# First batch's q loaded as rows of 34 tokens, and x put back in order on its way out of PSUM

## The chip, the cores and the metric

The kernel runs on one core of a Trainium2 chip. A core has TensorE (PE in the profile, with its weight loads shown as PEld), VectorE (DVE), ScalarE (ACT), GpSimd (POOL) and the queues that issue DMA transfers, here those of SyncE (SPq) and ScalarE (ACTq). The metric is the device time of one execution in microseconds; lower is better.

## The reference

Two blocks follow each other, for 4 batches of 1088 tokens. The first is a sketched linear attention with 4 heads of 32 columns:

```python
def phi(x):                       # S1, S2: 8 x 32, float64 in the inputs
    a = einsum('rd,bhsd->bhsr', S1, x)
    b = einsum('rd,bhsd->bhsr', S2, x)
    return einsum('bhsi,bhsj->bhsij', a, b)      # 64 features per token and head
q_p, k_p = phi(q), phi(k)
kv  = einsum('bhsf,bhsd->bhfd', k_p, v)
z   = sum(k_p, axis=2)
x   = einsum('bhsf,bhfd->bhsd', q_p, kv) / (einsum('bhsf,bhf->bhs', q_p, z) + 1e-6)
```

The four heads are laid side by side, so x is 1088 x 128 per batch. The second block is a mixture of 4 attention experts:

```python
logits = x @ w_gate                              # the two largest of 4 are chosen
w = softmax over the two chosen logits
for e in range(4):
    a = causal_softmax((x @ wq[e]) @ (x @ wk[e]).T / 8)
    out += (w of e, 0 where e is not chosen) * (a @ (x @ wv[e]) @ wo[e])
```

## The kernel before, in words

Every piece of work is a *job*: a function that issues a few instructions on one engine, with what it reads, what it makes and which buffers it holds. `ORDER` (line 22 on) is a list of job numbers written out by hand; `Plan.run` goes through it and issues the jobs in that order, so each engine's instruction stream, and each DMA queue's, is the list cut down to that engine. A letter behind a number picks one of two engines; a dummy matmul with a "b" is left out. Buffers of a pool are handed out in order of the list: there are four PSUM pairs (two banks each), three buffers for loaded and turned q and k, three for features, six general ones.

For each batch the work goes:

1. *Load* k, q, v. For batch 0 k comes as rows of 34 tokens: partition 32h + t holds tokens 34t to 34t + 33 of head h, each 32 columns, in two transfers of 2,048 and 2,304 bytes a partition (L424). q comes by head, in four transfers on two queues: partition t of a head holds tokens t, 32 + t, 64 + t and so on, in 34 runs of 128 bytes (`by_head`, L429). v of batch 0 comes as rows of 34 tokens too (L436, L440).
2. *Turn* (DVE): 32 x 32 blocks are transposed, so that the columns of a head stand on partitions. k's turn for batch 0 also puts the tokens in another order, with strided reads and writes of 256 columns (L489); q's goes straight (L495).
3. *Sketch* (PE, L519): 32 matmuls with 32 x 32 weights and 288 columns, for S1 and S2, four heads and four groups. Then DVE brings the result *back* (L523).
4. *Features* (DVE and POOL, L528): the 64 products, four jobs for q and four for k.
5. *Sums* over the tokens for k (PE, L559), kept by ACT or DVE.
6. For batch 0 (`attend_rows`): q's features are turned by PE in five pieces (L593) and copied out (L192), *numer* multiplies them with the sums (L616), *divide* divides on DVE (L623 to L625), *turn x* transposes x in three pieces (L631) and *keep x* copies each out of PSUM (L192). *Store x* writes each piece to DRAM (L644, L647) and *fetch x* reads it back in rows of 32 partitions for the values (L651).
7. *Choose experts*: logits by thirds (L808), turned back (L812), comparisons, choices (L833 to L849) and shares.
8. *Queries* (L961, base copies and predicated picks L974), *scores* (L999), exp (L1027), weights (POOL, L1042), turn (L1047), *values* (L1075), *outputs* (L1196).

The sketch matrices come as float64 and are decoded by integer operations on DVE (L303 to L318); PE meanwhile runs dummy matmuls on a zeroed tile (L248). Batch 1's preparation is interleaved with batch 0's choices and scores, and so on. Line 192 is the copy helper of all engines.

Of the kernel before, what the change touches and what calls it, by code (L numbers as in the profile page):

```python
# [10 lines left out]
F32 = mybir.dt.float32  # L11
# [10 lines left out]
1 16a 60 9a 13a 22a 24a 27a 77 5b 46 31a 12a 0 3 2 45 48 79 76 78 90 4 49 75 81 83 74 89 52 51 88 80 87 8a 50 98 99 47  # L22
64 54 100 91 102a 104a 84 101a 92 93 82 53 391 96a 103b 66 97a 19b 95a 85b 113 114a 94b 109 110a 393 59 117 118a 56
111 394 65 392 402 44a 55 115 86a 106 57 112b 63 105 67a 401 405 116b 395 58 108b 406 407 411a 397 399 107a 119 398
404 120 124 125 129 126 127a 130 400 121 61 7b 408a 122a 396 68 131 62a 146 132a 409a 412 147 70 410a 413 414a 69 150
148 403 71 152 153 151 154 149 169 415 128 167 416 420a 123 687 168 170 417 418a 155 17b 179 686 685 684 694 133 73 72
419a 162 163 180 184b 421 174 175 183a 164 422 424 423 430 425 426 139 156 157a 185 158 159a 182 181 246 245 186 187
194 431 137 171 172 249a 188 189 695 208 209 210 195 428a 427a 432 434a 433a 196 250a 222 223 688 160 161a 26b 25b 38b
201 165 429 202 224 203 319 215 197a 190b 251 198 216 225a 226 435 166a 199 200 247 227 248 698 252 228 268 204b 191
192 205 206 217 218a 219 176 220 135 173 700 699 267 269 270 318 323a 193 322a 436 438a 207 141 703a 271b 704b 437b  # L30
324 221 211a 212 260 261 262 263a 213 275 321 276 277 278 279b 177 178b 214 253 254 456 458 272 457 273 14b 142 693
320 325 255 292 291 293 274 701a 42b 264 691 280 702a 134 136 229 230 231 459 460 692 256b 234a 284 294 283 233a 462
281 257 232a 258 265 690 689 706 705 285 286 235b 342 707a 708 237 236 239 709 710 696 713a 238 711a 712a 259 282 697
461 266 295a 296 343 326 344 297 287a 327 328 288 289 298 714 715 717 463 350 290 329 330b 716 723 724 725 345 346a
10b 143 21b 472 138 331 473 477b 718 347 351 352 35b 353 354a 144 727a 332 348 719 140 29b 439 476b 464 299 300 301
302 303 304 308a 441 306a 307a 726a 333 349 467 478 335 310 474 440 334 305b 309 475 336 479 359 337 338a 358 360 339
361 362 355 468 508 509 442 720a 984 311 312 540 721a 363 340 501 364a 443 502 480 979 341 481 482 541 314 465 487 365
488 356 357 483a 315 313 366 367 538 494 977 978 495 980 316a 981 728 539 542a 368 369 370 987 496 503 504a 145 371
372 373 374 317 469 375 470 543a 544 545 471a 505 506 985 988 484 485 486 497b 444 498 722 499 510 511b 489 490a 491
512 513 376 379b 447 500 380a 515 383 516 553 377a 381 445 554 492 493 378a 382 448 584 585 586 517 518a 729 555 449  # L40
446 453 982 983 730a 514 519 731b 451 991 520 521 993 749 556b 992 994b 587 588a 569 546 996b 750 384 385 997a 507 557
558 547 751 548 386 568 989 522 589 523 524 549a 550 551 559 570 571 526a 752 753 590 242 591 525a 754 611 529 995a
530 241 528b 527a 531 612 616a 561 760 732 452 387 615a 755 455 466 733 572a 756 560 573 574 389 614 562 563 986 613
240 576 577 617 618 620 575 43b 552 532 644 619 578 28b 18b 579 621 243a 580b 581 643 765 652 564a 565 766 769a 582
651 768 757 645 583 636 566 567 390 653 770a 771 635 654 655 627 622 244 623a 761 762 628 637 656 657b 629 630 638 767
772 624 658 659 646 625 592 660 639a 640 631b 641 593 594 450 595 596 597 794 598a 999 647a 632 642 601b 602 648 600a
599a 795 633 634 649 998 736 1000a 603 605 535 626 454 773 774 787 650 534 763 788 533 780 781 808 809 810 811a 764a
536b 812 661 662 789 775 663 813 796 797b 798 790b 604 782 664 665 666 667 1002 814 668 669 990 1005a 734 776b 777
672a 671a 778 1006b 670b 1001 735 739 1003 832 1004a 791 388 799 783b 800 673a 674 675 831 835a 801 784 1007 802 803
1008 792 676 1009 793 836a 834 677 1010 1016 833 904 738 678 742 758 804b 1011 837 30b 1017 785 805 806 759 1012 1018  # L50
838 1013a 905 908a 862 1014a 1020a 909a 807 679 910 878 786 779 737 537 877 879 747 839 840 841 907 906 880 911 861
863 1019a 1021 881b 842a 846 847 682 740 815 816 817 746 864 865a 820a 853 866 867 821a 824 854 1015 868 882 936 819a
823 855 39b 34b 40b 41b 848 849b 937 818a 850 851 856 822 938 1022 1024b 869 1023b 607 843 883 884 939 870 748 871 872
# [62 lines left out]
def kernel(  # L116
# [177 lines left out]
    def decode():  # L294
# [8 lines left out]
        ve.tensor_scalar(out=ex, in0=hi, scalar1=20, scalar2=0x7FF, op0=SHR, op1=AND)  # L303
# [3 lines left out]
        ve.tensor_single_scalar(lw, lo, 29, op=SHR)  # L307
        ve.tensor_single_scalar(ex, ex, 255, op=ALU.min)
        ve.tensor_tensor(out=ma, in0=ma, in1=lw, op=OR)
        ve.tensor_single_scalar(S_hi, ex, 0, op=ALU.is_gt)  # L310
        ve.tensor_single_scalar(lw, lo, 0x1FFFFFFF, op=AND)
        ve.tensor_single_scalar(ex, ex, 23, op=SHL)
        ve.tensor_copy(last, lw)
        ve.tensor_tensor(out=sg, in0=sg, in1=ex, op=OR)
        ve.tensor_tensor(out=ma, in0=ma, in1=sg, op=OR)
        ve.scalar_tensor_tensor(out=S_lo, in0=last, scalar=2.0**-52, in1=sg.bitcast(F32), op0=ALU.mult, op1=ALU.mult)
        ve.tensor_tensor(out=S_hi, in0=ma.bitcast(F32), in1=S_hi, op=ALU.mult)
# [8 lines left out]
    job("decode", "DVE", 2.3, lambda e: decode(), ["raw"], "ST", [sroom], rank=-190)  # L326
# [89 lines left out]
    def prepare(b, rank):  # L416
# [3 lines left out]

        def load_k(eng, x):
            if early:
                c0, c1 = (0, 512, S)[x : x + 2]
                eng.dma_start(out=plan[kin][:, c0:c1], in_=k[b].rearrange("h (t c) d -> (h t) (c d)", c=C)[:, c0:c1])  # L424
            else:
                by_head(eng, plan[kin], k, x)
# [31 lines left out]
        for x in range(2 if early else 4):  # L458
            job(f"load k{b}.{x}", "SP", 0.45 if early else 0.7, lambda e, x=x: load_k(nc.sync, x), lead,
                ("kin", b, x if early else 0), [kin], landing=0.8 if early else 0.95, rank=rank(-0.1))  # L460
        def load_rows():

            nc.sync.dma_start(out=plan[qin][:, 0:S], in_=q[b].rearrange("h (t c) d -> (h t) (c d)", c=C))

        if early:
            for x in range(4):
                job(f"load q{b}.{x}", "ACT" if x % 2 else "SP", 0.42, lambda e, x=x: by_head(nc.scalar if e == "ACT" else nc.sync, plan[qin], q, x),
                    lead, ("qin", b), [qin], landing=0.85, rank=rank(-0.09))
# [10 lines left out]
        def turn_k(x):  # L479
# [8 lines left out]
            for g in range(2):  # L488
                nc.vector.transpose(d[:, :, 2 * x + g], s[:, :, 2 * x + g])  # L489
# [796 lines left out]
```

## Time and profile before

| | |
|---|---|
| median of 3 runs | 277.88 us (277.2 to 278.68) |
| profiled execution | 277.85 us, span 276.1 us |
| PE busy | 261.8 us (95%) |
| DVE busy | 217.5 us (79%) |
| POOL busy | 153.8 us (56%) |
| ACT busy | 99.4 us (36%) |
| DMA | 85,579 packets, 27.36 MB, 54,112 packets under 512 bytes |

Engine rows give the time in which an engine had an instruction in flight; waiting for something else is idle time, shown in brackets behind a row with what ended it. Matmul records come in pairs for each float32 matmul. SPq and ACTq rows are the issue of a transfer; the time to landing is given in the DMA rows. The chain of waits follows the work that ended last back to the start.

### The profile page before, as it was taken

Reading aid. Unit: us, or ns where it says so; the run is one execution under the profiler, and the core shown is the slowest. Engines: PE = TensorE matmul, PEld = TensorE weight load, DVE = VectorE, ACT = ScalarE, POOL = GpSimd, SP = SyncE. Lnnn points to the kernel's source line nnn. Section 1 sums busy time; section 2 is a strip of 40 time slices with the busy share of each in tenths; the row PEclk is TensorE's granted clock in tenths of the full one; section 3 lists DMA queues with packets and bytes.
Section 4 is the critical chain, followed back from the end, with each engine's and each line's share of the span. In section 5 each row is a group of like instructions: output and inputs, shape, how many; then the busy total and the mean of one; then the engine's idle time right before and its main releaser. Section 6 shows DMA issues by size and latency. Waiting matters only on the chain.

```text
span 276.1 us, 9491 instructions
## 1 busy us (share of the span) xinstructions
PE 261.8 (95%) x3961; PEld 193.7 (70%) x3961; DVE 217.5 (79%) x543; ACT 99.4 (36%) x271; POOL 153.8 (56%) x247
## 2 busy tenths in 40 slices
PE   7679998899999999989999999999999999999994
PEld 2367854457585796676589986665597975789994
DVE  3998689989989987998969437989899358995344
ACT  2030356344423444333462332462532425434110
POOL 5386358656789834546565448666348242652730
PEclk9999999999999999999999999999999999999999
DMA  7965739952607979143900165700412854940012
GB/s 158 183 144 82 156 91 205 165 72 60 125 20 116 193 193 170 37 103 68 198 6 4 30 151 130 176 2 2 101 47 51 154 121 104 171 81 2 5 32 52
DMA packets 85579, 27.36 MB, mean 99 GB/s; under 512 B 54112, under 2 KB 84896, under 8 KB 85536
## 3 DMA queue, kind: packets, MB, share of 16 engines
q1 hardware_dynamic: 83168, 26.41, 48.0%
q8 instruction: 31, 0.51, 0.8%
q10 hardware_dynamic: 2368, 0.35, 0.7%
q14 instruction: 12, 0.10, 0.1%
HBM read 22.22 MB, written 4.52 MB: 97 GB/s over the span
## 4 chain that ended last, share of the span: by engine, by line
PE 63%; DVE 22%; DMA 4%; issue 4%; ACT 3%; POOL 2%; SPq 1%; DVEq 0%; ACTq 0%; POOLq 0%
PE pair L1075 24%; PE pair L999 18%; PE pair L961 6%; PE pair L1196 6%; DVE AT L1047 3%; DVE w L1011 2%; DVE w L523 2%; DVE fp L528 2%; DVE qs L974 2%; DMA in<-in_k_dram 2%; DMA xra<-xd 2%; PE pair L1146 2%; PE pair L559 2%; PE pair L519 1%; PE pair L1172 1%
## 5 line engine op out<-in xcount | busy, mean ns | idle before, releaser
L1042 POOL TENSOR_SCALAR w<-w,rs,sh 128x896 f32<-128x896 f32 (+15 forms) x68 | 55.9, 829 | 55.0 <-DVE rs L1038 53.0
L999 PE MATMUL pair<-xT,qs 128*128 128x384 f32 (+11 forms) x216 | 76.4, 481 | 3.4 <-DVE agg L192 1.3
L1027 ACT ACTIVATE w<-w,mx 128x640 f32<-128x640 f32 (+15 forms) x68 | 52.4, 771 | 69.2 <-DVE mx L1011 54.1
L999 PEld LDWEIGHTS pair<-xT,qs 128*128 128x128 f32 x216 | 37.4, 190 | 28.7 <-issue 9.7
L1047 DVE STREAM_TRANSPOSE AT<-w 128x576 f32<-128x576 f32 (+14 forms) x68 | 50.7, 758 | 5.9 <-POOL w L1042 5.5
L1011 DVE CUSTOM_DVE_ANT_0 w<-pair,mask 128x768 f32<-128x768 f32 (+13 forms) x68 | 48.1, 719 | 6.5 <-PE pair L999 6.1
L1075 PEld LDWEIGHTS pair<-AT,xra 32*128 32x128 f32 x1136 | 41.6, 185 | 6.4 <-DVE mx L1011 2.6
L1075 PE MATMUL pair<-AT,xra 32*128 32x192 f32 (+5 forms) x1136 | 44.7, 303 | 0.2 <-DMA xra<-xd 0.2
L1102 POOL TENSOR_TENSOR agg<-agg,mb 128x768 f32<-128x768 f32 (+1 forms) x22 | 34.1, 1561 | 11.7 <-ACT agg L192 6.6
L961 PE MATMUL pair<-xT,Mq 128*128 128x384 f32 (+1 forms) x96 | 34.8, 476 | 0.3 <-DVE w L523 0.2
L528 POOL TENSOR_TENSOR fp<-w 128x576 f32<-128x576 f32 x23 | 27.1, 1194 | 8.2 <-DVE w L523 8.0
L192 ACT COPY agg<-pair 128x384 f32<-128x384 f32 (+1 forms) x34 | 14.5, 462 | 44.3 <-PE pair L1075 36.7
L1075 PE MATMUL pair<-AT,xrb 32*128 32x160 f32 (+5 forms) x752 | 26.9, 287 | 0.0
L1075 PEld LDWEIGHTS pair<-AT,xrb 32*128 32x128 f32 x752 | 26.4, 185 | 0.5 <-issue 0.4
L961 PEld LDWEIGHTS pair<-xT,Mq 128*128 128x128 f32 x96 | 17.3, 190 | 11.2 <-issue 3.1
L974 DVE COPY_PREDICATED qs<-mb,pair 128x768 f32<-128x768 uint16 (+1 forms) x24 | 23.0, 959 | 2.2 <-DMA mb<-md 1.4
L1196 PEld LDWEIGHTS pair<-Mo,agg 128*128 128x128 f32 x168 | 20.6, 192 | 2.4 <-issue 1.3
L1196 PE MATMUL pair<-Mo,agg 128*128 128x128 f32 x168 | 21.6, 278 | 0.0
L192 DVE COPY agg<-pair 128x384 f32<-128x384 f32 (+1 forms) x12 | 6.4, 533 | 12.7 <-PE pair L1075 7.6
L1035 POOL TENSOR_SCALAR rs<-zs 128x1 f32<-128x1 f32 x31 | 6.6, 213 | 17.0 <-ACT w L1027 13.9
L1098 DVE COPY_PREDICATED agg<-mb,pair 128x384 f32<-128x384 uint16 (+1 forms) x24 | 12.6, 547 | 4.0 <-ACT agg L192 3.9
L1038 DVE RECIPROCAL rs<-rs 128x1 f32<-128x1 f32 x68 | 8.8, 143 | 7.8 <-POOL rs L1035 5.9
(165 smaller groups left out, 308.5 us busy)
## 6 DMA issues: line engine op xcount, KB each, us to landing
mb<-md SPq DMA_DIRECT2D x7, 576.0 KB, 5.4
xrb<-xd SPq DMA_DIRECT2D x16, 192.0 KB, 3.9
xra<-xd SPq DMA_DIRECT2D x16, 192.0 KB, 4.7
xrc<-xd SPq DMA_DIRECT2D x16, 160.0 KB, 4.3
mb<-md SPq DMA_DIRECT2D x4, 480.0 KB, 4.9
in<-in_k_dram SPq DMA_DIRECT2D x12, 136.0 KB, 4.2
in<-in_q_dram SPq DMA_DIRECT2D x3, 544.0 KB, 6.0
xd<-w SPq DMA_DIRECT2D x12, 136.0 KB, 3.6
```

The source lines that it names most:

```text
L192: (nc.scalar.copy if eng == "ACT" else VEC[eng].tensor_copy)(o, i)
L528: VEC[e].tensor_tensor(out=f, in0=a[:, :, None, R : 2 * R].to_broadcast([128, NJ, R, R]), in1=a[:, :, 0:R, None].to_broadcast([128, NJ, R, ...
L961: nc.tensor.matmul(plan[ps[x]][:, y, 0:w], Mq[:, ((1, 2), (0, 3))[x][y]], plan[xT][:, 64 * t0 : 64 * t1], start=True, stop=True)
L974: nc.vector.copy_predicated(chosen(), rows(c), rows(plan[ps[x]]))
L999: nc.tensor.matmul(plan[p][:, y, 0 : c1 - c0], plan[qs][:, 128 * t : 128 * t + 128], plan[xT][:, c0:c1], start=True, stop=True)
L1011: nc.vector.tensor_tensor_reduce(out=o, in0=src, in1=msk, scale=-1.0, scalar=mx[:, b, i, x - 1 : x] if x else 3e38, op0=ALU.add, op1=ALU.m ...
L1027: nc.scalar.activation(out=a, in_=a, func=ACTF.Exp, bias=mx[:, b, i, last : last + 1], scale=-1.0, accum_out=zs[:, b, i : i + 1])
L1042: nc.gpsimd.tensor_scalar(out=a, in0=a, scalar1=rs[:, b, i : i + 1], scalar2=plan[("sh", b)][:, i : i + 1], op0=ALU.mult, op1=ALU.mult)
L1047: nc.vector.transpose(dst[:, 0 : keys // 32, t], plan[A][:, 0:keys].rearrange("p (j s) -> p j s", s=32))
L1075: nc.tensor.matmul(plan[Vk[g // 2]][:, g % 2, lo : 32 * nt], plan[(f"xr{j // 12}", b)][rows, j % 12], a[rows, j, lo:], start=(j == 0), sto ...
L1102: nc.gpsimd.tensor_tensor(out=a, in0=a, in1=plan[mb][:, 2 * x : 2 * x + 2, 0:w], op=ALU.mult)
L1196: nc.tensor.matmul(plan[p][0:m, 0, 128 * x : 128 * x + 128], plan[agg][:, e, 128 * x : 128 * x + m], Mo[:, e], start=(e == 0), stop=(e == ...
```

## The change

- q of batch 0 is loaded like k, as rows of 34 tokens, in two transfers, one on SP's queue and one on ACT's; k's second half moves to ACT's queue.
- The turns of k and q are both plain 512 and 576 column transposes in the order in which the data comes. The tokens of a group then stand in another order, and the sketch of batch 0 is issued in two cuts, one of 32 columns and one of 256, for k and for q.
- x therefore comes out with partition 32g + t, tile j holding token 34t + 8g + j. `keep x` writes it in token order with strided writes (one copy for the first two pieces, two for the last), and all logits wait for all three pieces.
- `store x` is four transfers by group (runs of 4 KB) and one job with two transfers for the last two tokens of each 34, all behind all three divides; each fetch of x waits for all stores.
- The decode of the sketch matrices has 13 instructions in place of 16.
- The first part of `ORDER` is new; from about job 420 of 1275 in the list it is the same. Six dummies are issued in place of ten. The mask is made later on POOL, all five copies of q's turned features are on ACT, the first memsets on DVE change places.

```diff
+        ve.tensor_scalar(out=ma, in0=hi, scalar1=0xFFFFF, scalar2=3, op0=AND, op1=SHL)
         ve.tensor_scalar(out=sg, in0=hi, scalar1=31, scalar2=31, op0=SHR, op1=SHL)
-        ve.tensor_scalar(out=ma, in0=hi, scalar1=0xFFFFF, scalar2=3, op0=AND, op1=SHL)
...
+        ve.scalar_tensor_tensor(out=sg, in0=ex, scalar=23, in1=sg, op0=SHL, op1=OR)
...
+        def by_rows(eng, dst, src, x):
+            c0, c1 = (0, 512, S)[x : x + 2]
+            eng.dma_start(out=dst[:, c0:c1], in_=src[b].rearrange("h (t c) d -> (h t) (c d)", c=C)[:, c0:c1])
...
-            job(f"load k{b}.{x}", "SP", 0.45 if early else 0.7, lambda e, x=x: load_k(nc.sync, x), lead,
+            job(f"load k{b}.{x}", ("SP", "ACT")[x] if early else "SP", 0.45 if early else 0.7,
+                lambda e, x=x: load_k(nc.scalar if e == "ACT" else nc.sync, x), lead,
...
-            for x in range(4):
-                job(f"load q{b}.{x}", "ACT" if x % 2 else "SP", 0.42, lambda e, x=x: by_head(...
+            for x in range(2):
+                job(f"load q{b}.{x}", ("SP", "ACT")[x], 0.42, lambda e, x=x: by_rows(...
...
-            s = src[:, 0 : 128 * N8].rearrange("p (g j d) -> p j g d", g=4, j=N8)
-            d = dst[:, 0 : 128 * N8].rearrange("p (j g t) -> p j g t", j=N8, g=4)
-            for g in range(2):
-                nc.vector.transpose(d[:, :, 2 * x + g], s[:, :, 2 * x + g])
+            cols = slice(512 * x, S if x else 512)
+            nc.vector.transpose(dst[:, cols], src[:, cols])
...
+            if early:
+                cuts = [(32 * N8, 32, lambda a, g: a[:, 128 * N8 + 32 * g : 128 * N8 + 32 * g + 32]),
+                        (0, 32 * N8, lambda a, g: a[:, 32 * N8 * g : 32 * N8 * g + 32 * N8])]
+            for o, w, part in cuts:
+                for s in range(2):
+                    for h in range(H):
...
         def keep_x(e, x0, x1, t):
+            o = plan[xT].rearrange("p (t c) -> p c t", c=C)
+            src = plan[t][:, 0, 0:384].rearrange("p (j g t) -> p j g t", g=4, t=32)
+            n = min(x1, N8) - x0
+            copy(e, o[:, 0 : 4 * N8].rearrange("p (g j) t -> p j g t", g=4)[:, x0 : x0 + n], src[:, 0:n])
+            if x1 > N8:
+                copy(e, o[:, 4 * N8 :], src[:, n, 0 : C - 4 * N8])
+
+        def store_x(g):
+            dst, x = xd[b].rearrange("(t c) d -> t c d", c=C), plan[xs].rearrange("p (j d) -> p j d", d=128)
+            nc.sync.dma_start(out=dst[:, N8 * g : N8 * g + N8], in_=x[32 * g : 32 * g + 32, 0:N8])
+
+        def store_last():
+            dst, x = xd[b].rearrange("(t c) d -> t c d", c=C), plan[xs].rearrange("p (j d) -> p j d", d=128)
+            for g in range(C - 4 * N8):
+                nc.sync.dma_start(out=dst[:, 4 * N8 + g], in_=x[32 * g : 32 * g + 32, N8])
...
-                    [("xd", b, piece[n])], ("xr", b, n), [(f"xr{n}", b)], landing=1.1, rank=at + 0.3)
-        pieces_of[b] = piece
+                    [("xd", b)], ("xr", b, n), [(f"xr{n}", b)], landing=1.1, rank=rank(0.9 + 0.1 * n))
+        pieces_of[b] = {n: 0 for n in range(3)}
```

More of the change, by code (lines that the diff above doesn't have):

```diff
@@ L27 @@
[L27 to L31, printed above, removed]
@@ L325 @@
     job("mask", "POOL", 1.2, lambda e: make_mask(), (), "mask", rank=-60)
-    job("decode", "DVE", 2.3, lambda e: decode(), ["raw"], "ST", [sroom], rank=-190)
+    job("decode", "DVE", 2.0, lambda e: decode(), ["raw"], "ST", [sroom], rank=-190)
     for h in range(1, 4):
@@ L465, in prepare @@
         if early:
[L466 to L468 removed]
+            for x in range(2):
+                job(f"load q{b}.{x}", ("SP", "ACT")[x], 0.42, lambda e, x=x: by_rows(nc.scalar if e == "ACT" else nc.sync, plan[qin], q, x),
+                    lead, ("qin", b, x), [qin], landing=0.8, rank=-198.5)
         else:
[L470 removed]
+            job(f"load q{b}", "SP", 0.45, lambda e: load_rows(), lead, ("qin", b, 0), [qin], landing=3.2, rank=rank(-0.09))
         for x in range(5):
```

139 lines of the change are left out of this document (58 added, 81 removed).

## The prediction

> **What bounds the kernel now.** I read first the stages (busy time of each engine per stretch), because a change to the first batch can only pay where TensorE (PE) has room.
>
> ```profile
> 0.00:6.60 6.60, 5.35 (x18) 2.02 (x18) 2.39 (x20) 1.73 (x3) 3.58 (x22) 1.00 0.79 157
> 6.60:33.40 26.80, 21.48 (x443) 16.58 (x443) 22.13 (x49) 5.12 (x14) 14.60 (x20) 1.00 0.73 137
> 33.40:61.40 28.00, 25.41 (x304) 13.93 (x300) 25.80 (x77) 13.76 (x41) 18.11 (x42) 1.00 0.83 141
> 61.40:276.10 214.70, 209.55 (x3205) 161.12 (x3204) 167.14 (x399) 78.82 (x213) 117.51 (x165) 1.00 0.41 87
> ```
>
> Columns: stretch, length, busy PE, its weight loads, DVE, ACT, POOL, granted clock, DMA share, GB/s. Up to 6.6 us PE runs only dummy matmuls. From 6.6 to 33.4 it idles 26.80 - 21.48 = 5.3 us, from 33.4 to 61.4 another 2.6 us, and then it is 97.6% busy to the end. From the queries of batch 1 on (about 76 us) every engine's order is unchanged. So what counts is how much earlier PE has finished the same work at that point; the rest slides along.
>
> The second view is the chain that ended last, over the start.
>
> ```profile
> 4.60 4.98 DMA in<-in_k_dram
> ...
> 11.70 3.82 DVE fp L528 x3
> ...
> 15.57 0.66 PE pair L593 x4
> ...
> 16.26 0.66 PE pair L593 x4
> ...
> 19.55 0.77 DVE in L483
> ...
> 21.56 1.48 PE pair L519 x55
> ```
>
> The start hangs on k's second transfer (issued 4.60, landed 9.60), since DVE turns k before it takes q's sketch back, and then on DVE's features and copies. The third is the timeline of the start and the steps after it.
>
> ```profile
> 0.91 0.27 DVE L241 MEMSET idle<- 128x256 uint32 x1 [0.91 <-PEq L1270]
> 1.24 5.35 PE L248 MATMUL pair<-idle 128*128 128x512 bf16 x18 [1.24 <-DVE warm L238]
> 1.27 0.41 SPq L234 DMA_DIRECT2D w<-in_S_dram  x1
> 3.42 0.29 DVE L303 TENSOR_SCALAR w<-w 32x32 int32<-32x32 int32 x1 [2.17 <-DMA w<-in_S_dram]
> 5.25 0.23 DVE L318 STREAM_TRANSPOSE SK<-w 32x64 f32<-32x64 f32 x1
> 6.54 1.37 DVE L495 STREAM_TRANSPOSE in<-in 128x576 f32<-128x576 f32 x2 [1.06 <-DMA in<-in_q_dram]
> 7.96 1.62 PE L519 MATMUL pair<-in,SK 32*32 32x288 f32 x64 [1.37 <-DVE in L495]
> 11.85 1.53 POOL L528 TENSOR_TENSOR fp<-w 128x576 f32<-128x576 f32 x1 [4.39 <-DVE w L523]
> 15.57 2.23 PE L593 MATMUL pair<-ident,fp 128*128 128x128 f32 x14 [2.64 <-DVE fp L528]
> 16.90 2.72 DVE L528 TENSOR_TENSOR fp<-w 128x576 f32<-128x576 f32 x3
> 18.82 2.47 PE L559 MATMUL pair<-vp,fp 128*64 128x33 f32 x72
> 23.09 4.23 PE L616 MATMUL pair<-kvz,fp 128*128 128x66 f32 x36
> 24.66 4.58 POOL L528 TENSOR_TENSOR fp<-w 128x576 f32<-128x576 f32 x4 [2.24 <-DVE w L523]
> 33.41 0.71 PE L394 MATMUL pair<-AT 64*128 64x128 f32 x8
> ```
>
> **The change part by part.** q's 4352 runs of 128 B become 256 runs of 2 KB and more. The DMA rows that price them:
>
> ```profile
> in<-in_k_dram SPq DMA_DIRECT2D x1, 288.0 KB, 4.9
> in<-in_q_dram SPq DMA_DIRECT2D x2, 136.0 KB, 3.6
> ```
>
> *Sketch matrices.* The big memset of the dummies' operand moves behind the small one the S loads wait for: issue at 1.27 - 0.27 = 1.0, arrival 3.42 - 0.27 = 3.15. The decode loses 3 of 16 instructions; 3.42 to 5.48 was 2.06 us, so 1.67 now: done at 4.8 instead of 5.5.
>
> *q and k.* q's halves are issued behind S on two queues at about 1.45 and 1.75. Bounds for a row transfer: the 3.6 us of the old q pieces and the 4.9 us of k's 288 KB half, which ran behind other traffic. With little ahead of it I take 3.6: q is in at 5.1 (6.7 at worst). The two turns (1.37) with the small copy end at 6.6, against 7.9. k's first half is issued fourth on SP, at about 2.35, and with 4.9 us is in at 7.25; its turns become contiguous (0.35 us less of DVE). They end at 8.65, under q's sketch.
>
> *The sketches of q and k.* Each is now cut in two: 64 records of 256 columns and 64 more of 32. The present 64 took 1.62 us; less the last one's 0.40 that is 19.2 ns a record.
>
> ```profile
> L519 PE MATMUL pair<-in,SK x224: 401/401/426, 8.0 to 37.5; 32*32 32x288 f32 x112
> ```
>
> If the records are paced by issue, the added 64 cost 64 x 19.2 = 1.23 us; if by columns, nothing (64 x (256 + 32) is the old sum). Nearer is the issue price, since the weight loads double too: q's sketch runs 6.65 to 9.5. The sketch of q is on the path; k's mostly waits for DVE anyhow. For the same step the Trainium skill ("TensorE: Matmul & The Clock Gate", section "Wait — 56ns, not 53.3ns?") says that start-to-start never drops below about 25 ns however few the columns. The 19.2 ns above are already below that, so row and page differ; by the page the 128 records would take 3.2 us and the gain below would shrink by some 0.7 us.
>
> *Features.* DVE takes q's second half back at 9.5 to 10.2 and then runs 2 features instead of 3 before k's turn, POOL two. With POOL busy beside it a DVE feature takes 3.82 / 3 = 1.3 us, and POOL's takes 1.53. DVE: 10.2, feature to 11.5, back to 12.2, feature to 13.5; POOL ends at 13.7. q's features are complete at 13.7, against 15.5. k: backs to 14.9, two features at 1.1 (between 0.91 = 2.72 / 3 and 1.3) to 17.1; POOL's two end at 16.6. Against 16.90 + 2.72 = 19.6 that is 2.5 us earlier.
>
> *Turns, sums, numerators.* The five turns of q's features need PSUM pairs that k's backs free (14.2, 14.9), so they run 13.9 to 16.7; all five copies go to ACT, idle then, which takes two copies off DVE. The sums follow, the last half from 17.1 on, to 19.1 (before 21.3). Batch 1's k turns (0.77 us the one in the chain) no longer stand between copies, so its sketch runs at once, 19.1 to 20.7, and the numerators 20.7 to 24.95 (before 27.3). The last divide ends 1 us behind them, at 25.95.
>
> *x out of PSUM in order.* The copies now write with a stride of 34 words, as batch 1's already do:
>
> ```profile
> L192 ACT COPY xT<-pair 128x512 f32<-128x512 f32 x1 | 1.1, 1130 | 0.0
> L192 ACT COPY fp<-pair 128x512 f32<-128x512 f32 x2 | 1.2, 586 | 10.6 <-PE pair L593 10.5
> L192 DVE COPY xT<-pair 128x64 f32<-128x64 f32 x1 | 0.3, 293 | 0.0
> ```
>
> 1130 against 586 ns for 512 columns: about 1.06 ns more a column. The last piece (256 + 64 columns) takes 0.38 (half of 586, with the fixed part) + 256 x 1.06 ns + 0.29 = 0.94 us on ACT. All logits now wait for all three pieces: turn 0.55, copy 0.94, ready at 27.5. The three logits take 1.4 us to 28.9, and batch 1's sums (2.3) end at 31.2; they need POOL's four features of k1 (4.58 us), which start when k1's first half is back (21.4, behind its sketch) and have two constant jobs of some 2.5 us among them: 28.5, just in time. Before, PE had done this very set when it began L394 at 33.41. So PE is **2.2 us ahead** here. Storing x also becomes all or nothing (six transfers, 4 KB runs), but from 26 us; the fetches serve the values' sums only at 61 us.
>
> *Between 31 and 77 us* the jobs are newly ordered, same work. DVE is further ahead than PE: its last turn of choices ends at about 33.4 instead of 36.25, and the queries' second pick at about 37 instead of 42.3 with some 1.3 us less of other work done by then, so 4 us.
>
> ```profile
> 35.92 0.33 DVE cTa L887
> ...
> 41.30 1.03 DVE qs L974
> ```
>
> With DVE ahead of PE some of the 2.6 us that PE idles there should go; I take 0.4. What could be late next is the fetched x:
>
> ```profile
> L651 SPq DMA_DIRECT2D xra<-xd x4: 422/689/3181, 36.0 to 51.7; - x4
> ...
> DMA to landing us min/median/max: 3.3/4.8/6.4
> 61.42 3.11 PE pair L1075 x78
> ```
>
> The last is issued at 51.7 and in by 58.1 at the latest; the sums start at 61.42, later 58.8. DMA is 83% busy from 33.4 to 61.4, and v of batch 2 now stands ahead of it (some 1.8 us), but the masks that begin the stage go out some 4 us earlier. It holds.
>
> **Sum.** 2.2 + 0.4 = 2.6 us. The profiled execution took 277.85 us (span 276.1), the median of the runs is 277.88: 275.2.
>
> **Rivals.** *Cold array.* Six dummies replace nine at the start. The rows of PE show 18 records from 1.24 to 6.59: the weight loads start 0.42 us apart up to 3.35, and 11 more take 2.32 us from 3.78.
>
> ```profile
> 3.35 0.15 PEld L248 LDWEIGHTS <-idle 128*128 128x128 bf16 x1 [0.28 <-issue]
> 3.78 2.32 PEld L248 LDWEIGHTS <-idle 128*128 128x128 bf16 x11 [0.28 <-issue]
> ```
>
> So 12 records now end at about 5.1, 1.5 us before q's sketch, 3 us if q lands at 6.7. If the array is slow again by then, q's sketch takes up to twice as long, and with what follows some 1.6 us of lead go: 276.8. Against it, after the 2.64 us of idle before 15.57 the first four L593 took 0.66 us, as did the next four at 16.26. The rule of the Trainium skill ("TensorE: Matmul & The Clock Gate", "What's actually happening") is half the clock after one idle window of about 3.4 us; by that rule the gap of 1.5 us costs nothing, and no row here shows a longer one. Chance 0.08.
>
> *Lead lost in the middle.* PSUM pairs or the DMA hold PE between 37 and 61: the x fetches land 2.5 us later than I sum, or the picks wait for masks. PE then starts its sums at about 61 as before: 277.5, within 0.5%. DMA at 0.83 speaks for it, DVE's lead against. Chance 0.12.
>
> *Slower: POOL between the turns of batch 1.* The mask (0.95 us and its two selects) leaves POOL's start and now stands between the shares and batch 1's query weights, so that DVE's inversions wait for POOL and POOL's scaling for DVE, twice, before two last POOL features and turn L736, which PE's numerators wait for in order.
>
> ```profile
> 5.92 0.95 POOL L284 MEMSET mask<- 128x1024 bf16 x1
> ...
> 43.98 2.31 POOL L528 TENSOR_TENSOR fp<-w 128x576 f32<-128x576 f32 x2
> 47.96 1.36 DVE L736 STREAM_TRANSPOSE fp<-fp 128x1152 f32<-128x1152 f32 x1
> ```
>
> The features ended at 46.3; I sum to about 47.0, the turn to 48.4, PE there at 49. If POOL comes more than 0.6 us later than that, PE stands; at 4.6 us the kernel is 1.4 us slower, and at 6 it ends at 280. POOL is 65% busy from 33.4 to 61.4 (18.11 of 28), so it would take long waits. Chance 0.15.
>
> **Chances and range.** Forecast 0.60 (273.5 to 276.4 by its own bounds: sketch price 0 to 1.9 each, DMA 3.6 to 4.9, up to 1.5 more if PE follows DVE's 4 us). A case in which it follows DVE fully, 273 or less, 0.05. Both are faster; the three rivals stand at 0.08 (276.8), 0.12 (277.5), 0.15 (280). The run-to-run band, 277.2 to 278.68, makes 0.5% (1.4 us) about what can be told from no change: faster below 276.5, slower above 279.3. Faster 0.65, same 0.20, slower 0.15. The range reaches from 273.0 to 278.4, which leaves out most of the slow rival and the far end of the gain.
>
> **What would show it.** Right: q's turn at about 5.1, k's wait gone, q's sketch near 2.85 us, last x copy at 27.5, batch 1's sums ending near 31.2, first score near 37.5, first values' sums near 58.8. Wrong: q's turn after 6.5, a sketch of 3.5 us or more, a PE idle of over 3 us between 33 and 60, or the values' sums waiting for fetched x.

## The result, and the profile after

The changed kernel takes 273.84 us (median of 6 runs, 273.02 to 274.71) against 277.74 us (276.96 to 278.68) for the kernel before: a ratio of 0.986, with a 95% interval of 0.9828 to 0.9891. The forecast was 275.2 with a range of 273.0 to 278.4; the gain is 3.9 us where 2.6 were summed. The profiled execution took 274.27 us, span 272.5. The medians given below leave out one execution each of plain_keep (276.94) and copies_on_dve (282.97), which ran in a slower state of the chip, over 1.5% above the fastest of the same kernel.

First the stages of the changed kernel, cut where PE has done the same work as at the cuts of the kernel before (columns as there).

```profile
0.00:31.20 31.20, 27.08 (x582) 19.32 (x582) 23.02 (x66) 8.69 (x19) 17.29 (x39) 1.00 0.76 157
31.20:58.99 27.79, 25.90 (x297) 14.21 (x296) 24.28 (x70) 15.08 (x44) 20.59 (x46) 1.00 0.85 135
58.99:74.25 15.26, 15.26 (x268) 10.24 (x264) 14.72 (x43) 5.97 (x16) 10.45 (x14) 1.00 0.31 66
74.25:272.50 198.25, 193.13 (x2941) 150.63 (x2940) 153.06 (x360) 72.24 (x196) 105.53 (x150) 1.00 0.43 89
```

The first stage ends 2.2 us earlier than before (31.2 against 33.4), the second another 0.2 earlier (58.99 against 61.4, so 2.4 in all). The second group of values begins at 74.27 here and at 76.92 before, 2.65. The last stage brings one more microsecond, which makes 3.6 in the profiles.

Next the chain of waits of the changed kernel, over its start.

```profile
2.33 5.92 DMA in<-in_k_dram
...
8.34 1.37 DVE in L481 x2
9.71 0.68 DVE w L520
```

It still begins with a transfer of k, as before: only its issue is now at 2.33, not 4.60. Then the timeline of the same kernel, with the rows that answer to those quoted before.

```profile
1.31 5.17 PE L248 MATMUL pair<-idle 128*128 128x512 bf16 x12 [1.31 <-DVE idle L241]
2.88 0.17 DVE L303 TENSOR_SCALAR w<-w 32x32 int32<-32x32 int32 x1 [1.62 <-DMA w<-in_S_dram]
5.74 0.78 DVE L485 STREAM_TRANSPOSE in<-in 128x576 f32<-128x576 f32 x1 [1.33 <-DMA in<-in_q_dram]
6.58 0.77 PE L516 MATMUL pair<-in,SK 32*32 32x32 f32 x64
6.77 0.71 DVE L485 STREAM_TRANSPOSE in<-in 128x512 f32<-128x512 f32 x1
7.54 1.50 PE L516 MATMUL pair<-in,SK 32*32 32x256 f32 x64 [0.19 <-DVE in L485]
8.34 1.37 DVE L481 STREAM_TRANSPOSE in<-in 128x512 f32<-128x512 f32 x2 [0.86 <-DMA in<-in_k_dram]
9.64 0.74 DVE L520 STREAM_TRANSPOSE w<-pair 128x576 f32<-128x576 f32 x1
14.11 3.54 DVE L525 TENSOR_TENSOR fp<-w 128x576 f32<-128x576 f32 x2
20.78 4.23 PE L613 MATMUL pair<-kvz,fp 128*128 128x66 f32 x36
25.71 1.79 ACT L192 COPY xT<-pair 128x384 f32<-128x384 f32 x3 [5.87 <-PE pair L628]
28.90 2.34 PE L556 MATMUL pair<-vp,fp 128*64 128x33 f32 x72
38.05 0.49 POOL L720 TENSOR_TENSOR w<-w 128x144 f32<-128x144 f32 x1 [0.51 <-DVE w L520]
```

q is turned at 5.74 (before 6.54), its sketch ends at 9.04, k's turns hold DVE until 9.71, the numerators begin at 20.78 (before 23.09), x is in order at 25.71 + 1.79 = 27.50, batch 1's sums end at 31.24. The last row belongs to the mask and is used below.

### The profile page after: what moved, and what is told of

It reads as the page before. It is cut to its first block, busy times and chain, and to the rows that moved or that the text cites. A ratio compares the mean times of both kernels' runs of the same rounds, so it can differ in the third digit from the quotient of the medians.

```text
span 272.5 us, 9727 instructions
## 1 busy us (share of the span) xinstructions
PE 261.4 (96%) x4081; PEld 194.4 (71%) x4081; DVE 215.1 (79%) x534; ACT 102.0 (37%) x274; POOL 153.9 (56%) x248
## 4 chain that ended last, share of the span: by engine, by line
PE 73%; DVE 14%; DMA 6%; issue 3%; ACT 1%; POOL 1%; SPq 1%; DVEq 0%
PE pair L1073 27%; PE pair L997 21%; PE pair L959 8%; PE pair L1194 6%; PE pair L556 2%; DMA xra<-xd 2%; PE pair L1144 2%; DMA in<-in_k_dram 2%; DVE fp L525 2%; DVE w L520 2%; PE pair L516 2%; DVE w L1009 1%; DVE AT L1045 1%; PE pair L1170 1%; PE pair L756 1%
## 5 line engine op out<-in xcount | busy, mean ns | idle before, releaser
L1040 POOL TENSOR_SCALAR w<-w,rs,sh 128x384 f32<-128x384 f32 (+15 forms) x68 | 56.9, 844 | 56.2 <-DVE rs L1036 53.9
L1025 ACT ACTIVATE w<-w,mx 128x384 f32<-128x384 f32 (+15 forms) x68 | 52.4, 771 | 72.0 <-DVE mx L1009 64.8
L1045 DVE STREAM_TRANSPOSE AT<-w 128x576 f32<-128x576 f32 (+15 forms) x68 | 50.9, 759 | 6.1 <-POOL w L1040 5.5
L1009 DVE CUSTOM_DVE_ANT_0 w<-pair,mask 128x768 f32<-128x768 f32 (+14 forms) x68 | 48.2, 719 | 6.4 <-PE pair L997 5.9
L1073 PE MATMUL pair<-AT,xra 32*128 32x160 f32 (+5 forms) x1136 | 44.2, 302 | 0.0
L525 POOL TENSOR_TENSOR fp<-w 128x576 f32<-128x576 f32 x24 | 28.9, 1219 | 6.9 <-DVE w L520 6.9
L192 ACT COPY agg<-pair 128x384 f32<-128x384 f32 (+1 forms) x32 | 13.7, 461 | 42.1 <-PE pair L1073 34.5
L192 DVE COPY agg<-pair 128x384 f32<-128x384 f32 (+1 forms) x14 | 7.5, 536 | 12.7 <-PE pair L1073 7.5
L1033 POOL TENSOR_SCALAR rs<-zs 128x1 f32<-128x1 f32 x30 | 6.4, 214 | 15.7 <-ACT w L1025 12.8
```

Of the source, the lines that this page charges most:

```text
L192: (nc.scalar.copy if eng == "ACT" else VEC[eng].tensor_copy)(o, i)
L525: VEC[e].tensor_tensor(out=f, in0=a[:, :, None, R : 2 * R].to_broadcast([128, NJ, R, R]), in1=a[:, :, 0:R, None].to_broadcast([128, NJ, R, ...
L1009: nc.vector.tensor_tensor_reduce(out=o, in0=src, in1=msk, scale=-1.0, scalar=mx[:, b, i, x - 1 : x] if x else 3e38, op0=ALU.add, op1=ALU.m ...
L1025: nc.scalar.activation(out=a, in_=a, func=ACTF.Exp, bias=mx[:, b, i, last : last + 1], scale=-1.0, accum_out=zs[:, b, i : i + 1])
L1040: nc.gpsimd.tensor_scalar(out=a, in0=a, scalar1=rs[:, b, i : i + 1], scalar2=plan[("sh", b)][:, i : i + 1], op0=ALU.mult, op1=ALU.mult)
L1045: nc.vector.transpose(dst[:, 0 : keys // 32, t], plan[A][:, 0:keys].rearrange("p (j s) -> p j s", s=32))
```

## The experiments

All were timed in five rounds beside the kernel before, in three groups of four, each group on one chip; the kernel before took 277.94, 277.84 and 277.81 there. Kernels whose name begins with before_ are edits of the kernel before, the others of the changed kernel. The columns on the right are read off each profile: q's first turn, the first *back* of q, the first numerator, the end of batch 1's sums, the first values' sums, and the idle time of PE between the last two (the brackets of PE's rows, added up). In the kernel before and its two edits two of the three logits still follow batch 1's sums (to 33.41 in the kernel before), in the others none does, so that the stretch from "sums 1" to "values" can't be compared straight across.

| kernel | us | ratio, 95% | q turn | back | numer | sums 1 | values | idle |
|---|---|---|---|---|---|---|---|---|
| before | 277.74 | | 6.54 | 10.30 | 23.09 | 32.75 | 61.35 | 2.6 |
| changed | 273.84 | 0.9828 to 0.9891 | 5.74 | 9.64 | 20.78 | 31.24 | 58.99 | 1.7 |
| after_again | 273.62 | 0.9819 to 0.9862 | 5.27 | 8.94 | 20.69 | 31.15 | 57.87 | 0.6 |
| q_by_head | 275.28 | 0.9885 to 0.9943 | 6.53 | 10.15 | 21.72 | 32.18 | 59.89 | 1.6 |
| k_before_w0 | 273.17 | 0.9806 to 0.9849 | 5.31 | 8.64 | 19.64 | 30.10 | 57.78 | 1.6 |
| mask_early | 273.65 | 0.9828 to 0.9879 | 5.78 | 9.64 | 20.79 | 31.25 | 58.21 | 0.9 |
| plain_keep | 273.96 | 0.9852 to 0.9931 | 5.36 | 9.22 | 20.37 | 30.82 | 57.55 | 0.6 |
| one_cut | 273.79 | 0.9826 to 0.9879 | 5.25 | 9.11 | 20.25 | 30.71 | 57.99 | 1.2 |
| before_decode | 277.95 | 0.9985 to 1.0022 | 6.76 | 10.52 | 24.36 | 33.77 | 62.35 | 2.6 |
| before_k_early | 276.56 | 0.9934 to 0.9974 | 6.05 | 9.33 | 22.17 | 31.82 | 60.42 | 2.6 |
| copies_on_dve | 274.28 | 0.9858 to 0.9893 | 5.59 | 9.36 | 20.93 | 31.38 | 58.51 | 1.1 |
| features_split_before | 273.35 | 0.9826 to 0.9855 | 5.56 | 9.32 | 20.30 | 30.75 | 56.98 | 0.3 |
| no_dummies | 272.95 | 0.9808 to 0.9843 | 5.67 | 9.88 | 20.74 | 31.19 | 57.42 | 0.4 |
| k_early_few_dummies | 272.17 | 0.9785 to 0.9822 | 5.54 | 9.10 | 20.44 | 30.90 | 57.13 | 0.4 |

One profile is one execution: the landing of q alone moves by half a microsecond between two executions of the same kernel (changed and after_again). Differences of some 0.4 us between single profiles are therefore no evidence. More moves where PE runs slow for a while: in before_decode's profile the granted clock between 14 and 22 us is 0.79 (1.00 in the kernel before), and from q's *back* to the numerators it takes 13.84 us against 12.79, though the edit touches nothing there.

**after_again.** The changed kernel once more, as the yardstick of its group.

> The changed kernel once more, as the base of the runs beside it. Expected 273.8 us (0.986 of before); its profile again shows PE at the first values' sums of group 1 (xra, 192 columns) about 2.7 us ahead of before, and 3 to 4 us ahead at the end.

The time repeats: 273.62. The lead of PE does not: at the second group of values, where 2.7 us were expected, it is 3.78 (73.14 against 76.92), and at the end 4.1.

**q_by_head.** q's rows are taken back, everything else of the change stays.

```diff
-                lambda e, x=x: by_rows(..., plan[qin], q, x)
+                lambda e, x=x: [by_head(..., plan[qin], q, h) for h in (2 * x, 2 * x + 1)]
...
-77 7b 48 49 88 76 4
+77 7b 76 48 49 88 4
```

> The changed kernel with q of batch 0 loaded by head again, in runs of 128 bytes, two heads on each queue; everything behind it as in the changed kernel (q's tokens then stand in another order than k's, so x of batch 0 is another; the work is the same). Theory 1, the transfer is what counts: 544 KB at the 140 to 200 GB/s of the old start take some 1.5 us longer than as rows, q's turn starts near 7 instead of 5.74, k's near 9.8 instead of 8.34, and 1.2 to 1.7 us of the 3.9 go. Theory 2, the new order and the freed DVE and PSUM carry the gain: within 0.5 us of the changed kernel.

```profile
6.53 0.78 DVE L485 STREAM_TRANSPOSE in<-in 128x576 f32<-128x576 f32 x1 [2.34 <-DMA in<-in_q_dram]
...
10.15 0.74 DVE L520 STREAM_TRANSPOSE w<-pair 128x576 f32<-128x576 f32 x1
...
21.72 0.55 PE L613 MATMUL pair<-kvz,fp 128*128 128x66 f32 x3
```

The timeline of q_by_head: q's turn waits for its transfer to 6.53, as in the kernel before (6.54), and q comes back at 10.15 (10.30). It costs 275.28 - 273.62 = 1.66 us of the 4.3 gained in this group. That is the price of the rows with what hangs on them: four issues in place of two also put k's first half back on SP's queue, from 2.33 to 3.39, and in this profile the granted clock is 0.80 between 14 and 22 us, so that the turns of q's features take 3.40 us against 2.35 in the changed kernel. How much of the 1.66 each of these makes isn't told apart. The other 2.7 us are there without the rows: from q's *back* to the numerators it takes 11.6 us, before 12.8 (in the changed kernel 11.1), and more is won later.

**before_decode and before_k_early.** Two parts alone, put into the kernel before.

```diff
# before_decode: the 13-instruction decode of the changed kernel, and its small memset first
-1 16a 60 9a 13a 22a 24a 27a 77 5b 46 31a 12a 0 3 2
+0 1 16a 60 9a 13a 22a 24a 27a 77 5b 46 31a 12a 3 2
# before_k_early: k's first half (in time its second transfer) ahead of two of v's loads
-75 81 83 74 89
+75 74 81 83 89
```

> The kernel before with the short decode and the small memset ahead of the dummies' memset, as in the changed kernel; nothing else. The sketch matrices are ready some 0.6 us earlier. The chain before starts with k's second transfer (4.60 to 9.60), so nothing is expected at the end (within 0.3 us); if the decode were what the start waits for, 0.4 to 0.6 us less.

> The kernel before with k's second transfer issued right behind its first, ahead of two of v's, about 0.9 us earlier; nothing else. If the start is bound by this transfer: DVE takes q's sketch back at 9.7 to 10 instead of 10.37, and 0.4 to 0.9 us less at the end. If the rest of the gain of the changed kernel comes from q's transfer and the new order: under 0.3 us.

The decode alone gives nothing, 277.95: q's turn waits for q's transfer, not for S. k's first half alone gives 1.3 us, 276.56; this bears out the chain of the kernel before, which began with k. It is more than the 0.4 to 0.9 expected; in its profile q's first turn comes earlier too (6.05, not 6.54), and the numerators start 0.9 us earlier (22.17, not 23.09).

**k_before_w0.** In the changed kernel, k's first half is issued one place earlier on SP.

```diff
-76 4 52 51 74 75 56
+76 4 74 51 52 75 56
```

> The changed kernel with k's first half issued on SP ahead of the wq weights instead of behind them. In the changed kernel the chain starts with this transfer (issued 2.33, k's turn at 8.34), and DVE takes q's sketch back only behind that turn. Theory 1, this wait sets the start: k's turn 0.4 to 0.8 us earlier, q's sketch back at about 9.1 instead of 9.64, and 0.4 to 0.6 us less at the end. Theory 2, the start is bound by DVE and PE behind it: no change beyond 0.2 us.

k is turned at 7.09 instead of 8.34 (7.65 in after_again) and the numerators start at 19.64, one microsecond earlier than in both executions of the changed kernel. Of that the median keeps 0.45 (273.17 against 273.62), and the intervals overlap. So k's transfer still holds the start of the changed kernel, but what is won there is only partly kept.

**mask_early, one_cut, plain_keep.** Three costs that the forecast had suspected, each taken away.

```diff
# mask_early: the mask is made at POOL's start again
-22a 26b 2 46 77 ... 422 423 47 195
+22a 26b 2 46 47 77 ... 422 423 195
# one_cut: the sketch of batch 0 in one cut of 288 columns
-            if early:
+            if False:
...
# plain_keep: keep_x without the reordering
-            o = plan[xT].rearrange("p (t c) -> p c t", c=C)
...
+            t1 = min(128 * x1, S)
+            copy(e, plan[xT][:, 128 * x0 : t1], plan[t][:, 0, 0 : t1 - 128 * x0])
```

> The changed kernel with the mask made at the start of POOL again, where POOL waits for the sketch matrices (2.65 to 4.57), instead of between the shares and batch 1's weights. The rival of the prediction (POOL between the turns of batch 1 holds PE): turn L734 up to 1.5 us earlier and 0.5 to 1 us less at the end. Against it: in the changed kernel POOL waits 0.51 us for DVE behind the mask, so the mask is covered: no change beyond 0.2 us.

> The changed kernel with the sketches of batch 0 in one cut of 288 columns, as before the change (the columns are taken in another order; as many are computed). The prediction had the second cut at 1.23 us on the path for q. The changed kernel's trace has 64 records of 32 columns in 0.77 us, run while DVE still turns q's first half, and DVE turning k until 9.71 while q's sketch ends at 9.04: so no gain for q, and k's sketch shorter by 0.4 us under DVE's features. Expected within 0.2 us of the changed kernel; by the prediction's price 0.5 to 1.2 us less.

> The changed kernel with the three copies of batch 0's x out of PSUM plain, without the strided writes (x of batch 0 then keeps the order of the partitions; the reordering is left out). The prediction priced the last copy at 0.94 us against some 0.4 plain, on the way to all logits. If that is on the path: logits at about 27.4 instead of 27.84 and 0.3 to 0.5 us less at the end. If DVE or POOL is what the logits and sums wait for: within 0.2 us.

None gains anything that shows: 273.65, 273.79 and 273.96 against 273.62 and 273.84. The strided copies do cost ACT what was summed. By shapes, in the changed kernel and then in plain_keep (group, count, busy us, mean ns, idle before):

```profile
L192 ACT COPY xT<-pair 128x384 f32<-128x384 f32 x1 | 0.9, 890 | 5.9 <-PE pair L628 5.9
```

```profile
L192 ACT COPY xT<-pair 128x384 f32<-128x384 f32 x1 | 0.5, 478 | 5.9 <-PE pair L628 5.9
```

890 against 478 ns, on a step whose gain the time does not show. The times of plain_keep scatter too much (272.71 to 275.97) to settle 0.4 us, but the profiles do: in both kernels the logits start 1.68 us after the last turn of x begins (26.16 and 27.84 in the changed kernel, 25.75 and 27.43 in plain_keep). PE has other work until then (L352 and L391 in the changed kernel), and x in order at 27.50 is not what it waits for. With one_cut q's sketch takes 1.60 us in one piece but starts only when both halves are turned (7.05, 0.77 behind the start of the second turn); in two cuts the small one runs while DVE turns the other half (rows 6.58 and 6.77 of the changed kernel above).

**copies_on_dve and features_split_before.** Two candidates for what is won between q's *back* and the numerators: 1.65 us in the changed kernel (11.14 against 12.79), of which 1.3 are there at the end of the sums (19.33 against 21.29, each from its *back*) and 0.35 behind them.

```diff
# copies_on_dve: two copies of q's turned features back on DVE, behind batch 1's k turns
-13b 110a 63 114a 94a 104 58 391 402 401 405 406
+13b 63 94a 104 58 391 402 110b 401 405 114b 406
# features_split_before: one q job and one k job of the features from POOL to DVE
-100b 99a ... 91 95b 67a
+100a 99a ... 91 95a 67a
```

> Two of the five copies of q's turned features go back to DVE, one behind each turn of batch 1's k, as in the kernel before (0.65 us each there). Theory A (the lead is what the numerators' start gains, and DVE's queue sets it): batch 1's sketch starts at about 19.9 instead of 19.25 and the numerators at about 21.3 instead of 20.8, batch 1's sums end at about 31.7, and the time is about 0.5 us over the changed kernel's, 274.2. Theory B (only the transfers of q and k count): 273.7, numerators at 20.8.

> One q job and one k job of the features go from POOL to DVE, so that POOL has 1 + 1 of the 8 as in the kernel before, and DVE 3 + 3. Theory A (the rest of the gain, beyond the transfers, comes from how features are shared): q's features end at about 14.5, k's at about 18.7 instead of 17.65, numerators at about 21.8 instead of 20.8, first values' sums 1 us later, and the time is about 274.7. Theory B (only the transfers count): POOL and DVE slow each other, so that two on each side gain nothing, and the time stays at 273.7.

copies_on_dve: batch 1's sketch has to wait for DVE again, which in the timelines of the changed kernel it does not.

```profile
19.40 1.59 PE L516 MATMUL pair<-in,SK 32*32 32x288 f32 x64 [0.35 <-DVE in L481]
```

The wait is 0.35 us; from *back* to the numerators it takes 11.57 us against 11.14 in the changed kernel. The time is 0.4 to 0.7 us longer (274.28 against 273.84 and 273.62), with overlapping intervals. This agrees with theory A in place; the size, about 0.4 us, is no more than the scatter of single profiles.

features_split_before: theory A falls. Six features on DVE and two on POOL, as before, are no slower than four and four; the time is 273.35. The groups by shape for DVE's features of batch 0, from the kernel before, the changed one and this one:

```profile
L528 DVE TENSOR_TENSOR fp<-w 128x576 f32<-128x576 f32 x6 | 6.6, 1153 | 0.0
```

```profile
L525 DVE TENSOR_TENSOR fp<-w 128x576 f32<-128x576 f32 x4 | 5.2, 1325 | 0.1
```

```profile
L525 DVE TENSOR_TENSOR fp<-w 128x576 f32<-128x576 f32 x6 | 5.0, 865 | 0.1
```

Six cost 5.0 us here, 6.6 in the kernel before, and four cost 5.2 in the changed one. So the number of features on DVE alone does not set the time; what POOL does beside them seems to. In the kernel before POOL also copied v then (1.58 us for 128 x 1024 at 13.32), a copy that the change gives to ACT. That this copy is what most of the 1.3 us are made of fits the rows, but no kernel moved it alone; it stays an inference.

**no_dummies and k_early_few_dummies.** The cold array, and a better start.

```diff
# no_dummies
-42a 16a 8a 5a 22a 26b ... 56 21a 87
+42b 16b 8b 5b 22b 26b ... 56 21b 87
# k_early_few_dummies: four dummies, and k's first half ahead of w0
-42a 16a 8a 5a 22a 26b ... 76 4 52 51 74 75
+42a 16a 8a 5b 22b 26b ... 76 4 74 51 52 75
```

> All dummy matmuls of the start are left out. Theory A (12 records at 0.43 us did not change the array's pace in the changed kernel, so they do nothing there): q's second cut takes 1.5 us as before, numerators at 20.8, 273.7. Rival (cold array): q's sketch takes up to twice as long, 3 us and more for the second cut, q's result is taken back 1 to 1.5 us later, and the time is 274.7 to 275.3.

> k's first half is issued ahead of w0 as in k_before_w0 (273.2 there), and four dummies are issued instead of six, so that PE is free before q's second turn ends. If the dummies held PE at the start, q's sketch starts up to 0.1 us earlier and the time is 273.1; if the array needs them, the sketch is slower by 0.5 us or more and the time is 273.7 or above.

The sketches by line, in the changed kernel and then without dummies (durations in ns, least, median, most):

```profile
L516 PE MATMUL pair<-in,SK x256: 185/292/398, 6.6 to 12.2; 32*32 32x256 f32 x65, 32*32 32x32 f32 x63
```

```profile
L516 PE MATMUL pair<-in,SK x256: 208/436/631, 6.5 to 13.0; 32*32 32x256 f32 x66, 32*32 32x32 f32 x62
...
  DVE w L520: 0.4, 1
```

Without dummies the array is slow for both sketches: the longest record takes 631 ns instead of 398, q's sketch 3.34 us in all. Yet q is taken back at 9.88, 0.24 us later, DVE waits for k's sketch 0.4 us, the numerators start at 20.74 as in the changed kernel, and the time is no longer (272.95). The rival's mechanism exists; its price here is covered, because DVE is busy with k's turns until 9.75 anyway (q's sketch ends at 9.84) and the features of q and k fill the time after. Its profile is also one of the three without the last wait of the middle stage, described in the next section, so the median says little about the start. By the rule of the Trainium skill ("TensorE: Matmul & The Clock Gate", "What's actually happening") an array that has stood idle runs at half the clock until some 3.4 us of work have passed. The trace agrees in direction, 1.6 times on the longest record, but not in length: k's sketch, which begins at 10.38, 3.9 us after the first record and with PE busy in between, is as slow (longest record 629 ns).

k_early_few_dummies is the fastest kernel of the study: 272.17 us, 0.9803 of the kernel before with an interval of 0.9785 to 0.9822, below the changed kernel's 0.9828 to 0.9891 and just touching after_again's 0.9819 to 0.9862. Neither outcome that was expected came: the array is slow (granted clock 0.60 from 7 to 14 us), and yet the time is shorter. The start did not gain by it. Beside k_before_w0, which differs from it by the two dummies alone, DVE now stands 0.42 us for q's sketch instead of 0.18, and the numerators start at 20.44 instead of 19.64; from q's first turn on that is 14.90 us against 14.33. What makes up for this in the profiles is the middle stage, 26.23 us against 27.68, which ran without the last wait described in the next section.

## Why the prediction was right, and where it was off

**Up to batch 1's sums it held within 0.1 us, but two steps in it were off and cancelled, which is luck.** S was 0.4 us ahead of the sum (decode done at 4.4 instead of 4.8). q's transfers took 3.5 and 4.1 us from issue to landing, against the 3.6 taken, so the first turn came at 5.74, not 5.1 (ACT's half, issued at 1.75 by the forecast, had 5.35 by its own figures), and the second ended at 7.48, not 6.6. k's first half took 5.9 us, not 4.9, and its turns ended at 9.71, not 8.65; "they end under q's sketch" was wrong, and so was the sign "k's wait gone": DVE stands 0.86 us for k, and the chain still begins there. On the other side the second cut of q's sketch was priced at 1.23 us on the path, from 19.2 ns a record. It cost nothing: the 64 records of 32 columns took 0.77 us in all, under DVE's turn of the other half, and one_cut gains nothing. So q came back at 9.64 instead of 9.5, held by k's turns and not by the sketch.

**From there each sum came out within 0.6 us, and most within 0.1.** q's features 13.86 (13.7 foreseen), k's 17.65 (17.1), sums to 19.33 (19.1), numerators 20.78 to 25.01 (20.7 to 24.95), x in order 27.50 (27.5), logits to 28.97 (28.9), batch 1's sums to 31.24 (31.2). Its later signs came too: the first score at 37.16 (37.5), the first values' sums at 58.99 (58.8). A cause was missed within it: the prediction named the features' split, the copies and batch 1's turns as what frees DVE. The split gains nothing (features_split_before), the copies gain some 0.4 us (copies_on_dve), and POOL's copy of v, which went to ACT, was not named at all.

**The term "with DVE ahead of PE some of the 2.6 us that PE idles there should go; I take 0.4" came out as 0.2 us in the profiled execution, and as 1.2 and more in others.** PE's rows in that stage, first the kernel before:

```profile
38.68 0.49 PE L907 MATMUL pair<-cTa,AT 64*128 64x192 bf16 x4 [0.38 <-DVE w L523]
39.34 2.85 PE L961 MATMUL pair<-xT,Mq 128*128 128x384 f32 x8 [0.18 <-DVE w L523]
42.37 1.79 PE L999 MATMUL pair<-xT,qs 128*128 128x64 f32 x8 [0.18 <-DVE qs L974]
46.28 0.81 PE L999 MATMUL pair<-xT,qs 128*128 128x320 f32 x2 [0.59 <-ACT mb L192]
50.46 1.24 PE L999 MATMUL pair<-xT,qs 128*128 128x288 f32 x4 [0.55 <-DVE qs L974]
55.71 0.81 PE L999 MATMUL pair<-xT,qs 128*128 128x320 f32 x2 [0.71 <-ACT rs L1033]
```

These are 2.59 us, at the same six places in both edits of the kernel before. Then the changed kernel, complete as well:

```profile
48.48 1.20 PE L756 MATMUL pair<-fp,kvr 32*32 32x288 f32 x41 [0.25 <-DVE rs L1036]
...
52.25 0.75 PE L997 MATMUL pair<-xT,qs 128*128 128x288 f32 x2 [0.17 <-ACT xT L192]
...
56.45 1.56 PE L997 MATMUL pair<-xT,qs 128*128 128x384 f32 x4 [1.25 <-DVE in L485]
```

All six waits of the kernel before are gone, 0.42 us is new, and one last wait of 1.25 us stands before a score. The idle time thus falls by 0.9 us, but the stage gets only 0.2 us shorter: the same work, from 33.41 in the kernel before and from 31.24 in the changed one to the first values' sums, takes 27.94 and 27.75 us. Part of what was idle has become busy time (25.90 against 25.41 us in the stage rows): batch 1's numerators and the sketch beside them, 64 records each, take 1.77 and 1.60 us in a row in the kernel before, and 3.90 us in pieces, without the wait, in the changed one. The last wait is not a fixed cost. The same kernel executed again, and the kernel without dummies:

```profile
55.33 1.56 PE L997 MATMUL pair<-xT,qs 128*128 128x384 f32 x4 [0.22 <-issue]
```

```profile
53.32 3.12 PE L997 MATMUL pair<-xT,qs 128*128 128x288 f32 x10
```

It ranges from nothing (three kernels, whose stage then takes 26.23 us from batch 1's sums to the values) over 0.2, 0.5 and 0.7 to 1.25 us. So the middle is worth 0.2 us in the profiled execution of the changed kernel, 1.2 in after_again (26.72 us) and 1.7 at most, where 0.4 was taken; a fixed size for it was the wrong form of the term. The profile names DVE's turn L485 for it in two executions, a read of DVE in two more and nothing in four; the waiting score reads the result of neither, and in after_again it starts at 55.33, before this DVE turn does. Its cause stays open.

**"The rest slides along" is the other step that was off.** From the first to the second group of values, where the same work stands in another order, the kernel before and its edits take 15.57 us, the changed kernel and its edits 15.27 to 15.30. From the second group of values to the end the kernel before takes 199.2 us, its two edits 198.9 each, the changed kernel and its edits 198.0 to 198.9. In the profile of the kernel before one wait for fetched x lies on the chain late in that stretch:

```profile
172.16 4.97 DMA xra<-xd
```

The changed kernel's profiled execution lacks it; after_again has it at 168.14 and still takes 273.62. Its place on the chain is thus no property of the change, and where these 0 to 1.2 us come from isn't settled. The profiled executions are thus 3.6 us apart by 2.2 at the start, 0.2 in the middle, 0.3 and 1.0 behind it; for after_again it is 2.3, 1.2, 0.3 and 0.3, which makes 4.1. What the forecast of 2.6 lacked lies in the last three, and it divides differently from one execution to the next.

**The rivals.** Cold array: the mechanism is there when dummies go, and to a lesser degree in after_again. Its price depends on what else holds the start. From q's first turn to the numerators it takes 15.04 us in the changed kernel and 15.07 without dummies, but 15.42 in after_again and, with k early, 14.90 against 14.33. The gap of 1.5 us that the forecast set before q's sketch did not exist: the dummies did not speed up and ended at 6.48, 0.1 us ahead of it. And that the first eight L593 ran at their pace behind 2.64 us of idle time was weaker evidence than the forecast made of it: in before_decode the first eight do so too, and the next six weight loads take 1.14 us instead of 0.64. Lead lost in the middle: the fetched x was in time, as argued; PE's row at 58.99 shows no wait. Slower through POOL and the mask: POOL ran the mask at 36.0 to 37.5 while it would otherwise have waited; its first query weight starts at 38.05 (row above), 0.51 us after the mask, when DVE's result comes, and with the mask made early at 38.06. PE's numerators of batch 1 start at 47.2, before the 49 that was summed. (By the steps given there a delay of 6 us ends at 280.7, not 280.)

## What to carry to other kernels

Where two transfers feed one engine, move the one that the chain begins with, and read the chain again afterwards: here q was made faster and k still set the start, and moving k's issue in a queue gained 1.3 us in the kernel before, where the shorter decode gained nothing. A cost that is real on its engine (the strided copies, the second cut) is worth nothing in time until it is shown which other work it outlasts; and the answer can change with the next edit, as it did for the slow array once k came early. And idle time that goes from an engine's rows is not yet time saved: six waits of 2.59 us went at once here, and the same work took 0.2 us less in one execution and 1.2 in another.

## What the runs showed of the hardware

*DVE and POOL slow each other.* In the changed kernel a DVE feature that runs beside POOL's two takes from 14.11 to about 16.9, 2.8 us, and the next, when POOL is done with them, 0.75:

```profile
16.91 0.75 DVE L525 TENSOR_TENSOR fp<-w 128x576 f32<-128x576 f32 x1
```

The prediction had taken 1.1 us for each. The Trainium skill ("GPSIMD Engine Reference", "1. Specifications") says that POOL shares its interface to SBUF with DVE and contends with DVE instructions that have two SBUF inputs, as these have. The trace agrees, with a factor of up to 3.7, though one feature, at 10.41, took 0.76 us while POOL had begun its own at 10.53.

*Small records on 32 x 32 tiles.* 64 records of 32 columns took 0.77 us, 64 of 256 columns 1.50 us: at most 12 and 23 ns a record. The floor of about 25 ns that the prediction weighed doesn't hold for them. The Trainium skill ("TensorE: Matmul & The Clock Gate", "Measured speedup vs the span model") gives about 4 ns of issue for each further tile of the array, to which the 12 ns are nearer.

*Dummies and the clock.* The twelve records of the changed kernel stay 0.43 us apart to the end, while the kernel before's sped up after 3.78; the sketch behind them ran at its usual pace all the same. In after_again, the same kernel, a part of the sketches was slow (longest record 629 ns) and the granted clock between 7 and 14 us was 0.87. With four dummies it was lower still; the stages of k_early_few_dummies:

```profile
0.00:7.00 7.00, 4.23 (x72) 1.66 (x72) 3.30 (x19) 1.73 (x3) 2.08 (x16) 1.00 0.68 208
7.00:14.00 7.00, 6.81 (x213) 4.25 (x202) 6.12 (x9) 1.07 (x1) 3.97 (x4) 0.60 0.86 149
14.00:30.00 16.00, 15.51 (x285) 13.66 (x284) 12.37 (x32) 6.21 (x15) 11.35 (x20) 0.96 0.80 153
```

A clock of 0.60 for 7 us, in the fastest kernel of the study: its start takes some 0.6 us longer than that of k_before_w0 (14.90 against 14.33, above), and the end doesn't show it. In the kernel without dummies, whose sketches are as slow, the clock is shown as 1.00 from the first instruction on, so that there only the records' lengths tell it.
